# A gated linear-attention block on one core: the first phase in another order, its weight rounds spread anew, the attention's tiles reordered

## The chip, the core and the metric

The kernel runs on one core of a Trainium2 chip. The metric is the device time of one execution in microseconds (us); beside it stands the median over repeated runs. The engines are called as in the profile: PE (TensorE, matrix products), PEld (its weight loads), DVE (VectorE), ACT (ScalarE), POOL (GpSimd) and SP (SyncE, which here issues nearly all DMA transfers). Every engine works its own queue in order; so does SP, and a transfer that must wait for its data holds up those issued behind it.

## What is computed

The reference, cut to what matters, with x of 2048 x 576, 32 heads of 18 and a hidden width of 4608:

```python
xn = layernorm(x)                                   # eps 1e-5, no scale
q, k, v = split_heads(xn @ wqkv)                    # wqkv 576 x 1728
phi = lambda t: where(t > 0, t + 1, exp(t)) + 1e-6
kv = einsum("bhsd,bhse->bhde", phi(k), v)           # one state for all tokens
z  = einsum("bhsd->bhd", phi(k))
o  = einsum("bhqd,bhde->bhqe", phi(q), kv) / (einsum("bhqd,bhd->bhq", phi(q), z)[..., None] + 1e-6)
s  = merge_heads(o) @ wo                            # wo 576 x 576
g  = silu(gelu(x @ w1 + b1) @ w2 + b2)              # w1 576 x 4608, w2 4608 x 576
out = x + s * g
```

The state needs all tokens before any output of the attention can be formed: first a pass over all tokens (phase 1), then the attention tile by tile, then the two-layer network (FFN), which takes most of the time.

## The kernel before

**Products.** Every fp32 operand of a product is split into a rounded high part (a cast, mostly on ACT) and a low part (raw minus high, mostly on DVE); a product is done as high x high, low x high and high x low. The large products use a seven-product scheme on 2 x 2 blocks: sums and differences of blocks are formed for both operands, seven products replace eight, and the results are put together from PSUM. `ORDER_X` (line 149) gives the order of the products of a token pair: 2, 1, "e2", "sa", 6, "sb", "e5", 7, 5, 4, 3, where "e2" and "e5" are remainders of the contraction and "sa", "sb" are the state products (phi(k) times v) of the pair before.

**Phase 1 (lines 540 to 1111).** The 2048 tokens are 16 tiles of 128 in 8 pairs. Pairs 0 and 1 are written out by hand (648 to 745) as eight plain products, x00 to x11, with the loads, the splits of wqkv (`split_w`, 316), the sums of wqkv's blocks (`w_sum`, 322: T3, T1, T2, T4, two halves each, on POOL) and their rounding (`w_hi`, `w_lo`, 329 to 336) between them. Pairs 2 to 7 go through `phase1_pair` (868) and `products` (802). `products` issues the matmuls in the order above and calls a hook after each; the hooks carry the other work: for the pair itself phi of k (`phi_hi` three ACT operations, `phi_max` on DVE), the adds that put k, v and q together, and three `snapshot`s (800, ACT copies of a PSUM bank that the next product then overwrites, so PE waits for them). For the coming pairs the steps of preparation are: `load_x` (tile of x), `statistics` (189, DVE; the power on POOL), `share_stats` (230, mean and 1/deviation stored to DRAM), `load_stats` (234, read back as a broadcast tile bc), `load_xt` (245, the transposed x into R, which has two buffers), `center` (253, POOL subtracts the mean), `scale` (257, DVE), `x_sums` (263, DVE), the rounding `rest_hi`/`x_hi_ops` (ACT) and `rest_lo`/`x_lo_ops` (DVE), and the stores `store_rest`, `store_ops` (1792 KB of operands a pair, used again by the FFN). In pairs 6 and 7 only k and v are computed; their q products follow as `products(6, "q")` and `products(7, "q")` (981 to 1111).

When pair p runs, in the kernel before, statistics are made for pair p + 2 in the hook "e2", centring for pair p + 2 in hook 7, scaling, sums and rounding for pair p + 1 in hooks 2 to "sb". Pair 2 is an exception: most steps for pair 3 run in its own hooks 7 and 5.

**Weight rounds (460 to 538).** Between its other work the kernel prepares operands of the FFN's weights and stores them to DRAM: 5 We rounds (load 256 KB, store 896 KB) and 9 W2 rounds (load 864 KB, store two times 576 KB). A round is load, `round_sums` (POOL in phase 1, DVE in the attention), `round_hi` (ACT), `round_lo` (DVE), `round_store`, which also issues the next load. The raw tile has one buffer, so the rounds are one chain. Phase 1 does one round in each of pairs 3 to 7 (sums after product 1, hi after "sb", lo and store after 7) and one in the q products; the attention does sums at even tiles j, the rest at odd ones (1451 to 1454).

**Transition (1049 to 1164).** `make_zb` and `fold_wo` fold wo into the state; `split_kw` (1162) rounds the result into kw_h and kw_l. The last state product, the masking of the state and the first tiles' q handling stand here. zb, a broadcast row of sums that POOL multiplies with q (`by_sums`), is copied on POOL behind two tiles' work.

**Attention (1166 to 1457).** Tile j, in the order of tiles `TO`, is one pass of `attend(j)`: 28 matmuls, a copy of the result, a store. Around it stand the load of q for j + 6, the transposition of p for j + 2 (`transpose_p`, PE, with ACT and DVE rounding it to th and tl), and by_sums, denominators and p_mult for j + 4. For the four first tiles (`RAW`) phi of q was not applied in phase 1 and is done here, four tiles ahead. `beside(j)` (1392) loads and prepares the FFN's first operands at fixed j, and the weight rounds run as above. `TO` is 12, 13, 0 to 11, 14, 15.

**FFN (1845 to 1955).** 18 steps of up and down products; the change touches none of it.

Of the kernel before, what the change touches and what calls it, by code (L numbers as in the profile page):

```python
# [24 lines left out]
KT = 5  # L25
# [22 lines left out]
def linear_attention_gated_ffn(ctx, tc, x, xT, wqkv, wo, w1, w1e, b1, w2, b2, out):  # L48
# [272 lines left out]

    def w_sum(name, k, eng):
# [4 lines left out]
        eng.tensor_tensor(raw_w[name][:, k], raw_w[a][:, k], raw_w[b][:, k], op=op)  # L327
# [161 lines left out]
    class WeRound:  # L489
# [21 lines left out]
        def store(self):  # L511
# [5 lines left out]
    rounds = [WeRound(0), W2Round(0), WeRound(1), W2Round(1), WeRound(2), W2Round(2), WeRound(3),  # L517
              W2Round(3), WeRound(4)] + [W2Round(c) for c in range(4, NC)]
# [39 lines left out]
    for t in (3, 4, 5):  # L558
        load_x(t)
# [71 lines left out]
    def sums_plain_lo(p):  # L631
        x_lo_ops(p, 2, 10)
        store_ops(p)
# [11 lines left out]
    dve, pool = nc.vector, nc.gpsimd  # L645

# [16 lines left out]
    normalize(1)  # L663
    transpose_x(1)
# [19 lines left out]
    tile_raw(1)  # L684
# [9 lines left out]
    w_sum("T1", 0, pool), w_sum("T1", 1, pool)  # L694
# [10 lines left out]
    load_xt(2)  # L705
    for t in (6, 7, 8, 9):
        load_x(t)
    w_sum("T2", 0, pool), w_sum("T2", 1, pool)
# [8 lines left out]
    store_rest(1)  # L717
    statistics(6), share_stats(6), statistics(7), share_stats(7)
    center(2)
    load_stats(6), load_stats(7)  # L720
    w_sum("T4", 0, pool), w_sum("T4", 1, pool)
# [5 lines left out]
    scale(2)  # L727
    x_sums(2)
    w_hi("T2", 0), w_hi("T2", 1)
    w_lo("T2", 0, dve), w_lo("T2", 1, dve)  # L730
    k11 = phi_plain(3, x12)
    k11()
    op_tiles(2)
    x13 = bank2("x13")
    plain_x(1, 1, 1, x13, THEN)
    rest_hi(2), x_hi_ops(2, 0, 14)
    rest_lo(2), x_lo_ops(2, 10, 14)
    values_plain(3, x13)
    x11 = bank2("x11")
    plain_x(1, 0, 1, x11, THEN)  # L740
    x_lo_ops(2, 0, 10)
    store_rest(2), store_ops(2)
    w_hi("T3", 0), w_hi("T3", 1)
    w_lo("T3", 0, dve), w_lo("T3", 1, dve)
# [57 lines left out]
    def products(p, part, hooks, before=None):  # L802
# [8 lines left out]
        for i in ORDER_X:  # L811
# [15 lines left out]
            elif i == "e5":  # L827
# [3 lines left out]
                if kv:  # L831
                    nc.vector.tensor_tensor(
                        as2(k_bufs[0]), kv_of(X0), as2(u)[:, :, :KV], op=ADD
                    )
                    phi_hi(f"k{p}0", as2(k_bufs[0]))
                if q:
                    add_q(T0, 0, X0, u, part)
            elif i == 7:
                product_x(p, 7, A, part, False, rest=False)
                snapshot(p, 0, A, part)  # L840
                if kv:
                    phi_max(f"k{p}0", k_bufs[0], as2(k_bufs[0]))
            elif i == 5:
# [3 lines left out]
                if q:  # L847
                    add_q(T1, 1, X1, u_all[p][0], part)
            elif i == 4:
# [18 lines left out]
    def phase1_pair(p):  # L868
# [3 lines left out]
        nxt = p + 2 if p + 2 < NPR else None  # L872
        qp = (2 * p - 2, 2 * p - 1) if 2 < p < NPR - 1 else ()

        def operands():
            scale(prep)
            store_rest(prep)
            x_sums(prep)
            op_tiles(prep)

        def operands_hi():
            rest_hi(prep), x_hi_ops(prep, 0, 14)

        def operands_lo():
            x_lo_ops(prep, 0, 7), x_lo_ops(prep, 7, 14)
            store_ops(prep)

        def next_statistics():
            if nxt:
                ts = 2 * nxt, 2 * nxt + 1  # L890
                for t in ts:
                    statistics(t), share_stats(t)
                for t in ts:
                    load_stats(t)

        steady = prep is not None and not first

        def h2():
            if steady:
                operands()  # L900
            if first:
                x_sums(1, rest=False)
            if qp:
                phi_q_hi(qp[0])

        def h1():
            if steady:
                operands_hi()
            if first:
                x_hi_ops(1, 2, 10)  # L910
                w_hi("T1", 0), w_hi("T1", 1)
            if qp:
                phi_q_max(qp[0]), store_q(qp[0])
            if p in ROUNDS:
                round_sums()

        def he2():
            if not first:
                next_statistics()
            else:  # L920
                sums_plain_lo(1)
                load_xt(3), load_xt(4)

        def hsa():
            if steady:
                rest_lo(prep)
            if first:
                w_lo("T1", 0, dve), w_lo("T1", 1, dve)

        def hsb():  # L930
            if steady:
                operands_lo()
            if first:
                w_hi("T4", 0), w_hi("T4", 1)
                w_lo("T4", 0, pool), w_lo("T4", 1, pool)
                center(3)
            if p in ROUNDS:
                round_hi()

        def h7():  # L940
            if nxt and not first:
                center(nxt)
            if first:
                operands()
                operands_hi()
            if p in ROUNDS:
                round_lo(), round_store()

        def h5():
            if qp:  # L950
                phi_q_hi(qp[1]), phi_q_max(qp[1]), store_q(qp[1])
            if first:
                rest_lo(prep), operands_lo()
                next_statistics()
# [3 lines left out]
        def h4():  # L958
            if first:
                center(nxt)  # L960
                round_load()

        if p + 3 < NPR:
            load_x(2 * p + 6), load_x(2 * p + 7)
        if nxt and not first:
            load_xt(nxt)
        if p >= NPR - 2:
            late_tiles(p + 2)
        if not first:
            pend.pop()()  # L970
        products(p, part, {
            2: h2, 1: h1, "e2": he2, "sa": hsa, "sb": hsb, 7: h7, 5: h5, 4: h4,
        }, p - 1)

    ROUNDS = range(3, NPR)
# [4 lines left out]

    pend.pop()()
# [3 lines left out]
    op_tiles(NPR)  # L985
    f = OPS[NPR].bitcast(F32).rearrange("p a b -> p (a b)")
    wo_sb = late["wo"] + [f[:, :D]]
    nc.sync.dma_start(wo_sb[4][: GROUPS[4][1]], wo[GROUPS[4][0] :, :])
    nc.sync.dma_start(b1c, b1)
    TO = [2 * NPR - 4, 2 * NPR - 3, *range(2 * NPR - 4), 2 * NPR - 2, 2 * NPR - 1]  # L990
    for i in range(2):
        q_of[i] = f[:, (i + 1) * D : (i + 2) * D]
        nc.sync.dma_start(q_of[i], q_dram[i])
    state(NPR - 1)
    kvz, sums_k, last_row, zb_first = (late[n] for n in ("kvz", "sums_k", "last_row", "zb"))
    mask = late["mask"]
    ln = GROUPS[-1][1]
    nc.vector.copy_predicated(kvz[:G, : 4 * G], mask[:G, :], ps_kv[0][:G, : 4 * G])
    nc.vector.copy_predicated(kvz[:ln, 4 * G : D], mask[:ln, :ln], ps_kv[1][:ln, :ln])
    nc.vector.copy_predicated(kvz[:ln, D:], mask[:ln, 8:ln], ps_kv[1][:ln, 8:ln])  # L1000
# [1012 lines left out]
```

## Time and profile before

| what | value |
|---|---|
| runs of the kernel, us | 1228.76, 1224.53; median 1226.64 |
| profiled execution, us | 1229.29 |
| its span, us | 1227.6 |
| mean granted clock of PE | 0.951 |
| DMA over the span | 284.93 MB, mean 232 GB/s |

The profile is of one execution. Its lines give busy times of each engine, what ended an engine's idle time (`<-` names the releaser, with the tile and the line), and the clock that the throttle granted to PE. In a timeline a row is start, length, engine, line, operation, output and inputs, and in brackets the idle time before it. In rows of groups the two numbers behind the bar are the total busy time in us and the mean of one in ns. A span's stage is read by cutting it where PE begins the next pair.

### The profile page before, as it was taken

Reading aid. Unit: us, or ns where it says so; the run is one execution under the profiler, and the core shown is the slowest. Engines: PE = TensorE matmul, PEld = TensorE weight load, DVE = VectorE, ACT = ScalarE, POOL = GpSimd, SP = SyncE. Lnnn points to the kernel's source line nnn. Section 1 sums busy time; section 2 is a strip of 40 time slices with the busy share of each in tenths; the row PEclk is TensorE's granted clock in tenths of the full one; section 3 lists DMA queues with packets and bytes.
Section 4 is the critical chain, followed back from the end, with each engine's and each line's share of the span. In section 5 each row is a group of like instructions: output and inputs, shape, how many; then the busy total and the mean of one; then the engine's idle time right before and its main releaser. Section 6 shows DMA issues by size and latency. Waiting matters only on the chain.

```text
span 1227.6 us, 17832 instructions
## 1 busy us (share of the span) xinstructions
PE 1107.6 (90%) x6492; PEld 1015.6 (83%) x6492; DVE 847.6 (69%) x1212; ACT 512.9 (42%) x858; POOL 470.5 (38%) x391
## 2 busy tenths in 40 slices
PE   7975798857545799999999999999999999999998
PEld 6875798746545598998899899899899899889988
DVE  7474775355463688888888889877557557647666
ACT  6442565435221445445445445543323323323433
POOL 4332433133321456446445544523423413413430
PEclk9988899978867899999999999999999999999999
DMA  5565668316799968657757856899777767667452
GB/s 205 151 169 152 213 199 261 135 48 207 227 345 361 344 255 316 231 190 296 269 185 262 302 182 232 304 406 357 229 255 227 228 222 221 221 217 235 156 166 104
DMA packets 121359, 284.93 MB, mean 232 GB/s; under 512 B 12598, under 2 KB 54582, under 8 KB 118712
## 3 DMA queue, kind: packets, MB, share of 16 engines
q1 hardware_dynamic: 121272, 283.80, 67.1%
q8 instruction: 51, 0.84, 0.3%
q14 instruction: 36, 0.29, 0.1%
HBM read 176.23 MB, written 106.64 MB: 230 GB/s over the span
## 4 chain that ended last, share of the span: by engine, by line
PE 65%; DMA 6%; DVE 3%; issue 2%; SPq 1%; ACT 0%; POOL 0%; DVEq 0%; ACTq 0%
PE pm L1632 31%; PE e L1493 9%; PE zy L1493 9%; PE a L1493 9%; PE b L1493 5%; DMA w2r<-w 3%; PE pd L1752 2%; DMA s_dram<-s 1%; DVE w2o L482 1%; DMA rq_dram<-wa_rest1s 0%; DMA wa_rest1q<-rr_dram 0%; DMA we<-w1e 0%; DVE den L1017 0%; DVE w2r L471 0%; DVE w2r L472 0%
## 5 line engine op out<-in xcount | busy, mean ns | idle before, releaser
L1638 DVE TENSOR_TENSOR macc<-pm,macc 128x576 f32<-128x576 f32 x218 | 163.7, 751 | 50.3 <-PE pm L1632 48.4
L1210 ACT CAST h_h<-g 128x512 fp32r<-128x512 f32 x204 | 121.8, 620 | 132.8 <-PE pm L1632 131.7
L1213 DVE TENSOR_TENSOR h_l<-g,h_h 128x512 fp32r<-128x512 f32 x204 | 161.9, 800 | 0.0
L1175 PE MATMUL ps_s<-kw_h,th 128*128 128x288 f32 x160 | 41.3, 345 | 56.5 <-DVE th L1130 45.8
L1598 POOL TENSOR_TENSOR mid<-g 128x512 f32<-128x512 f32 x34 | 44.0, 1293 | 108.9 <-ACT g L1501 108.9
L1175 PEld LDWEIGHTS ps_s<-kw_h,th 128*128 128x128 f32 x160 | 30.8, 227 | 58.3 <-issue 45.5
L1592 POOL TENSOR_TENSOR g<-g 128x512 f32<-128x512 f32 x34 | 54.9, 1615 | 49.7 <-DVE h_l L1213 28.4
L1501 ACT ACTIVATE g<-b,b1c 128x512 f32<-128x512 f32 x36 | 24.8, 690 | 102.8 <-DVE b L1519 102.7
L1256 POOL TENSOR_TENSOR w1raw<-w1raw 128x256 f32<-128x256 f32 x18 | 13.2, 736 | 128.1 <-ACT h_h L1210 68.4
L1510 ACT COPY mid<-a 128x512 f32<-128x512 f32 x36 | 21.1, 585 | 94.1 <-PE a L1493 94.1
L1493 PE MATMUL a<-h0f,wa 128*128 128x512 f32 x144 | 51.5, 398 | 5.7 <-ACT mid L1510 5.7
L1513 DVE TENSOR_TENSOR mid<-b,mid 128x512 f32<-128x512 f32 x36 | 24.8, 690 | 45.6 <-PE b L1493 39.8
L1595 POOL TENSOR_TENSOR g<-g 128x512 f32<-128x512 f32 x34 | 55.2, 1624 | 2.7
L1723 POOL TENSOR_TENSOR fin1l<-fin1h,fin1l 128x288 f32<-128x288 f32 x8 | 6.9, 866 | 117.9 <-DMA fin1l<-s_dram 42.6
L1493 PE MATMUL a<-h0r,wa 128*128 128x512 f32 x144 | 50.4, 390 | 0.0
L1213 DVE TENSOR_TENSOR h_l<-mid,h_h 128x512 fp32r<-128x512 f32 x34 | 48.9, 1439 | 1.2
L1025 POOL TENSOR_TENSOR vb<-q,den 128x576 f32<-128x576 f32 x14 | 19.3, 1377 | 74.9 <-DVE den L1021 64.6
L1501 ACT ACTIVATE g<-e,b1c 128x512 f32<-128x512 f32 x36 | 24.8, 690 | 51.3 <-DVE e L1526 51.3
L1589 POOL TENSOR_TENSOR g<-g 128x512 f32<-128x512 f32 x34 | 44.2, 1299 | 2.7
L1526 DVE TENSOR_TENSOR e<-e,mid 128x512 f32<-128x512 f32 x36 | 24.8, 690 | 22.3 <-PE e L1493 22.3
L1175 PE MATMUL ps_s<-kw_l,th 128*128 128x288 f32 x160 | 39.6, 334 | 0.0
L471 DVE TENSOR_TENSOR w2r<-w2r 128x576 f32<-128x576 f32 x6 | 4.5, 758 | 49.7 <-DMA w2r<-w 49.7
(1029 smaller groups left out, 3667.0 us busy)
## 6 DMA issues: line engine op xcount, KB each, us to landing
we<-we_dram SPq DMA_DIRECT2D x36, 448.0 KB, 3.9
x_dram<-OPS SPq DMA_DIRECT2D x8, 1792.0 KB, 8.4
w2raw<-w SPq DMA_DIRECT2D x10, 1152.0 KB
op<-w2o SPq DMA_DIRECT2D x18, 576.0 KB, 5.0
w1raw<-w SPq DMA_DIRECT2D x18, 512.0 KB, 12.1
op_a<-wa SPq DMA_DIRECT2D x18, 512.0 KB, 5.7
op_c<-wc SPq DMA_DIRECT2D x18, 512.0 KB, 9.5
op_d<-wd SPq DMA_DIRECT2D x18, 512.0 KB, 6.5
```

Of the source, the lines that this page charges most:

```text
L1175: nc.tensor.matmul(ps[:, h, :HD], st[:, k, :], w[:, k, h * HD : (h + 1) * HD], start=(i == 0), stop=(i == len(seq) - 1),)
L1210: nc.scalar.copy(pair[0], src)
L1213: eng.tensor_tensor(pair[1], src, pair[0].bitcast(F32), op=SUB)
L1493: nc.tensor.matmul(ps, st, mv, start=first and n == 0, stop=n == len(seq) - 1, skip_group_check=True,)
L1501: nc.scalar.activation(g, ps, AF.Gelu_apprx_tanh, bias=b1c[:, f : f + 1])
L1513: tt(u1_sb, B, m1_sb, op=ADD)
L1589: tt(src[5, pr], A(1, 0), A(1, 1), op=ADD)
L1592: tt(src[6, pr], src[5, pr], A(0, 0), op=SUB)
L1595: tt(src[3, pr], A(0, 1), src[6, pr], op=SUB)
L1598: tt(src[7, pr], A(0, 0), A(1, 0), op=SUB)
L1632: nc.tensor.matmul(ps[:, q, :HD], hs[p][st][:, cs], m[:, p, :], start=(n == 0 and i not in CHAIN), stop=(n == 5), skip_group_check=True,)
L1638: nc.vector.tensor_tensor(dst, src, dst, op=ADD)
```

## The change

It moves work; the arithmetic is the same except where named.

- Prologue and pairs 0, 1: loads of x from tile 5 on are issued one by one earlier; statistics are made and shared for pairs 2 and 3 earlier, and for pair 4 within pair 1 (a new helper `share`); the eight `w_sum`s and the two `w_lo` of T4 go from POOL to DVE; three splits of the second weight half are cast together ahead of tile 2's normalization; pair 1's sums and pair 2's roundings come earlier; `load_xt(2)`, `load_xt(3)` follow the operand stores; centring of pairs 2 and 3 is done here.
- Pairs 2 to 7: statistics for p + 3 in hooks 5 and 4, centring for p + 2 in hook 7, scaling and sums for p + 1 in hook 2; rounding for p + 1 in hooks 1 and "sa" for pairs 3 to 5, in "sb" and later otherwise. Phi of a k tile moves one hook later. Phi of stored q tiles: both tiles in hooks 2 and 1, for pairs 3, 4, 5 and 7.
- Weight rounds: order We0, W2-0, W2-1, We1, W2-2, W2-3, We2, We3, W2-4, We4, W2-5 to W2-8 (before: alternating to We4, then W2-4 to W2-8). A table `ROUNDS` places six whole rounds at (pair, hook); the seventh's sums stand in q product 6. In the attention the sums stand at odd j, the rest at even j.
- Transition: the last state products and the mask go into q product 6; zb's copy goes to ACT; `split_kw` is interleaved with the transpositions, and the denominators of tiles 2 and 3 come after the first two splits.
- Attention: `TO` is 13, 12, 4 to 11, 0 to 3, 14, 15.

```diff
-    for t in (3, 4, 5):
+    for t in (3, 4):
         load_x(t)
...
+    def share(t):
+        statistics(t), share_stats(t)
...
     k00 = phi_plain(0, x00)
+    for k in (0, 1, 4):
+        w_hi_plain(k, 1)
     normalize(2)
-    tile_raw(0)
+    load_x(6)
+    tile_raw(0), tile_raw(1)
     k00()
-    split_w(0, 1, dve)
-    statistics(3), offset(3)
-    split_w(1, 1, dve), split_w(4, 1, dve)
+    w_lo_plain(0, 1, dve)
+    statistics(3)
+    w_lo_plain(1, 1, dve), w_lo_plain(4, 1, dve)
+    offset(3)
+    share(4), share(5)
...
-    w_sum("T3", 0, pool), w_sum("T3", 1, pool)
     sums_plain(0)
     tile_hi(2)
+    normalize(3)
+    load_x(7)
+    load_x(8), load_x(9)
     k01()
...
+    load_stats(4), load_stats(5)
+    w_sum("T3", 0, dve), w_sum("T3", 1, dve)
+    sums_plain_hi(0)
     values_plain(1, x01)
-    sums_plain_hi(0)
-    statistics(4), share_stats(4), statistics(5), share_stats(5)
-    normalize(3)
+    w_sum("T1", 0, dve)
     sums_plain_lo(0)
-    load_stats(4), load_stats(5)
+    center(2)
+    w_sum("T1", 1, dve)
+    w_sum("T2", 0, dve), w_sum("T2", 1, dve)
...
+    QP = {p: (2 * p - 2, 2 * p - 1) for p in range(3, NPR - 2)}
+    QP[NPR - 1] = (2 * NPR - 6, 2 * NPR - 5)
+    SUMS, HI, END = (round_sums,), (round_hi,), (round_lo, round_store)
+    ROUNDS = {
+        (3, 2): SUMS, (3, "sb"): HI, (3, "e5"): END,
+        (3, 5): SUMS, (4, "q"): HI, (4, 1): END,
+        (4, "e5"): SUMS, (4, 7): HI, (4, 5): END,
+        (5, 2): SUMS, (5, "sb"): HI, (5, "e5"): END,
+        (5, 5): SUMS, (6, 2): HI, (6, 1): END,
+        (6, "e5"): SUMS, (7, "q"): HI, (7, 1): END,
+    }
...
-    TO = [2 * NPR - 4, 2 * NPR - 3, *range(2 * NPR - 4), 2 * NPR - 2, 2 * NPR - 1]
+    TO = [2 * NPR - 3, 2 * NPR - 4, *range(4, 2 * NPR - 4), *range(4), 2 * NPR - 2, 2 * NPR - 1]
...
-    products(NPR - 2, "q", {2: round_sums, 7: lambda: (round_hi(), round_lo(), round_store())})
+    products(NPR - 2, "q", {2: round_sums, "sb": masked_state, 4: first_phi}, NPR - 1)
...
-    nc.gpsimd.tensor_copy(zb[1], zb_first)
+    nc.scalar.copy(zb[1], zb_first)
...
-        if loaded and j % 2 == 0:
+        if loaded and j % 2:
             round_sums(dve)
         elif loaded:
             round_hi(), round_lo(), round_store()
```

The hooks of `phase1_pair`, after:

```python
def h2():
    if first: w_hi("T4", 0), w_hi("T4", 1)
    if prep: scale(prep), store_rest(prep), x_sums(prep), op_tiles(prep)
    for n, t in enumerate(qp[::-1]):
        phi_q_hi(t)
        if not n: rounds_at(p, "q")
def h1():
    if early: rest_hi(prep), x_hi_ops(prep, 0, 14)
    for t in qp[::-1]: phi_q_max(t), store_q(t)
def hsa():
    if first: w_lo("T4", 0, dve), w_lo("T4", 1, dve)
    if early: rest_lo(prep), x_lo_ops(prep, 0, 7), x_lo_ops(prep, 7, 14)
def hsb():
    if prep and not early: rest_hi(prep), x_hi_ops(prep, 0, 14)
def h7():
    if cent: center(cent)                 # cent = p + 2
    if early: store_ops(prep)
def h5():
    if stat: share(2 * stat), share(2 * stat + 1)   # stat = p + 3; then load_x of the next pair
def h4():
    if stat: load_stats(2 * stat), load_stats(2 * stat + 1)
    if first: round_load()
```

`load_xt(p + 2)` stands at the start of pair p, and `early` is true for pairs 3 to 5.

More of the change, by code (lines that the diff above doesn't have):

```diff
@@ L917, in he2 @@
[L917 to L932, printed above, removed]
+        cent = p + 2 if p + 2 < NPR else None
+        stat = p + 3 if p + 3 < NPR else None
+        qp = QP.get(p, ())
@@ L933, in hsb @@
+        early = 2 < p < NPR - 2
+        def h2():
             if first:
                 w_hi("T4", 0), w_hi("T4", 1)
[L935 to L938, printed above, removed]
-        def h7():
[L941 to L947, printed above, removed]
@@ new lines, in hsa, with hsb, he5 @@
+        def hsa():
+            if first:
+                w_lo("T4", 0, dve), w_lo("T4", 1, dve)
+            if early:
+                rest_lo(prep), x_lo_ops(prep, 0, 7), x_lo_ops(prep, 7, 14)
+        def hsb():
+            if prep and not early:
+                rest_hi(prep), x_hi_ops(prep, 0, 14)
+        def he5():
+            if first:
+                rest_lo(prep), x_lo_ops(prep, 0, 7), x_lo_ops(prep, 7, 14)
+                store_ops(prep)
+        def h7():
+            if cent:
+                center(cent)
+            if early:
+                store_ops(prep)
@@ L958, in h4 @@
         def h4():
+            if stat:
+                load_stats(2 * stat), load_stats(2 * stat + 1)
             if first:
-                center(nxt)
                 round_load()
[L963 to L966, printed above, removed]
+        if cent:
+            load_xt(cent)
         if p >= NPR - 2:
@@ L1420, in beside @@
                 w.hi(i), w.lo(i)
[L1422 to L1425 removed]
     RAW = range(4)
+    split_kw(0, dve)
+    transpose_p(0)
+    split_kw(1, dve)
+    transpose_p(1)
+    denominators(2), p_mult(2)
+    for k in range(2, KT):
+        split_kw(k, dve)
+    denominators(3), p_mult(3)
     load_q(4), load_q(5)
[L1430 to L1431 removed]
     pad(2)
```

192 lines of the change are left out of this document (87 added, 105 removed).

## The prediction

> **What bounds the kernel now.** I read the page first, then the span cut into stages by TensorE's work (the windows view), then TensorE's waits before 430 us, and last the timelines and the chain where those waits lie.
>
> ```profile
> span 1227.6 us, 17832 instructions
> PE 1107.6 (90%) x6492; PEld 1015.6 (83%) x6492; DVE 847.6 (69%) x1212; ACT 512.9 (42%) x858; POOL 470.5 (38%) x391
> ```
>
> TensorE is busy 90% of the span, so 120 us of it are idle. The windows say where; each row is a stretch, its length, busy time of PE, PEld, DVE, ACT and POOL, granted clock, DMA share and GB/s.
>
> ```profile
> 0.00:38.94 38.94, 32.05 (x147) 27.63 (x148) 30.26 (x49) 21.58 (x39) 17.99 (x21) 0.91 0.44 161
> 38.94:73.04 34.10, 25.41 (x138) 23.43 (x137) 16.93 (x27) 13.68 (x27) 15.22 (x10) 0.95 0.53 143
> 73.04:107.66 34.62, 25.97 (x121) 24.20 (x121) 22.82 (x39) 16.06 (x24) 7.74 (x6) 0.80 0.62 193
> 107.66:143.52 35.86, 24.09 (x121) 22.41 (x120) 16.65 (x33) 14.31 (x20) 12.12 (x11) 0.81 0.63 170
> 143.52:165.49 21.97, 21.97 (x122) 20.99 (x120) 16.61 (x34) 14.52 (x21) 8.52 (x6) 1.00 0.76 241
> 165.49:187.45 21.96, 21.96 (x121) 20.99 (x120) 15.54 (x33) 14.33 (x20) 6.59 (x8) 1.00 0.77 242
> 187.45:208.06 20.61, 17.29 (x121) 17.05 (x120) 14.57 (x23) 13.45 (x20) 7.42 (x19) 0.92 0.72 231
> 208.06:223.71 15.65, 15.65 (x123) 15.49 (x121) 4.74 (x8) 6.84 (x11) 1.75 (x4) 1.00 0.59 197
> 223.71:254.50 30.79, 26.14 (x150) 21.88 (x149) 13.02 (x27) 12.21 (x28) 8.01 (x6) 0.94 0.40 130
> 254.50:269.31 14.81, 1.48 (x12) 1.05 (x10) 6.67 (x14) 6.32 (x11) 5.74 (x5) 0.71 0.14 43
> 269.31:331.20 61.89, 46.87 (x297) 44.66 (x297) 36.22 (x63) 26.78 (x48) 21.69 (x15) 0.88 0.57 183
> 331.20:414.06 82.86, 43.87 (x249) 41.37 (x249) 39.33 (x54) 17.19 (x32) 18.69 (x14) 0.75 0.94 342
> 437.46:482.18 44.72, 44.72 (x269) 40.80 (x268) 39.18 (x52) 21.28 (x38) 23.44 (x20) 1.00 0.74 279
> ```
>
> The first two rows are the prologue and pairs 0 and 1 (the plain products); then one row for each of pairs 2 to 7, one for the two late q products, one for the transition, two for the attention, and one of the 18 FFN steps. Pairs 4 and 5 show the floor: the 121 matmuls of a whole pair take 21.97 us with TensorE full and the clock at 1.00. Pairs 2 and 3 take 34.62 and 35.86 for the same work. In the FFN TensorE is full: the change leaves it alone, so what is saved ahead of it reaches the end unshortened.
>
> ```profile
> PE ps_s L1175 <- DVE th L1130: 45.8, 8, 14.3
> PE xaall L361 <- ACT u L800: 11.8, 1, 11.8
> PE ps_s L1175 <- ACT kw_h L1163: 10.7, 1, 10.7
> PE x1all L361 <- DVE q L428: 8.6, 1, 8.6
> PE x0all L361 <- DVE kph L403: 6.7, 1, 6.7
> ```
>
> Those are TensorE's longest waits before 430 us (total, times, longest). The engine named is the last link; the timelines say what held it.
>
> ```profile
> 57.35 0.46 DVE L191 BATCH_NORM_STATS2 st<-x 128x6 f32<-128x288 f32 x1 [12.20 <-DMA x<-x]
> 96.38 2.89 DVE L259 TENSOR_TENSOR R<-R,bc 128x640 f32<-128x640 f32 x2 [6.11 <-DMA R<-xT]
> 120.38 3.82 POOL L255 TENSOR_TENSOR R<-R,bc 128x640 f32<-128x640 f32 x2 [12.22 <-DMA bc<-st_dram]
> ```
>
> VectorE's queue is in order. Ahead of pair 2 it stood 12.20 us on the load of a tile of x, in pair 2 6.11 us on the transposed x of pair 3, and in pair 3 GpSimd's centring stood 12.22 us on the broadcast statistics: three loads asked for too late, with TensorE behind each.
>
> **The change, part by part.**
>
> *Start of pair 2.* The loads of x are issued earlier, so the 12.20 goes. Against that, eight weight sums and two roundings move from GpSimd to VectorE.
>
> ```profile
> L327 POOL TENSOR_TENSOR raw<-raw,raw 128x864 f32<-128x864 f32 x8 | 19.1, 2415 | 0.0
> L320 DVE TENSOR_TENSOR wB22l<-raw,wB22h 128x864 fp32r<-128x864 f32 x2 | 2.0, 1054 | 0.0
> ```
>
> On GpSimd a sum of this shape takes 2.415 us, on VectorE 1.054 by the undisturbed row, so ten cost VectorE 10.5 us, eight of them (8.4) ahead of pair 2. By TensorE alone pair 2 can start at 32.05 + 25.41 = 57.5. VectorE does 30.26 + 16.93 = 47.2 there; with 8.4 that is 55.6, and to 58.5 with what comes forward from pair 2. I take 58.5 instead of 73.04, a gain of 14.5; the bound on the other side is 64, if half of VectorE's 12.20 returns on other loads.
>
> *Pair 2.* Transposed loads and centring come two pairs ahead, so the 6.11 goes. VectorE's work there is 22.82, plus two roundings, 2.1, minus what went ahead: about 24 against TensorE's 22. I take 24, so pair 3 starts at 82.5 (before: 107.66).
>
> *Pair 3.* Statistics are stored and read back three pairs ahead, not two; the 12.22 is covered by a whole pair, 21.97. I take 23 instead of 35.86; pair 4 starts at 105.5.
>
> *Pairs 4 and 5.* Here nothing was to gain and something is added. The weight rounds go from one a pair to six in three and a half pairs, with their sums on GpSimd ahead of the centring and their casts on ScalarE ahead of the snapshots for which TensorE waits. The transfers exist in before; only their times move. For two rounds whose load may land late in the pair I add 0.5 and 2.5; the bounds are 0 and 2.5 for each pair. Pair 6 then starts at 105.5 + 43.9 + 3 = 152.5 (before: 187.45).
>
> *Pairs 6, 7 and the q products.* Pair 6 does pair 7's work in 17.29 busy at clock 0.92; I take 15.65 + 1, then 15.65 for pair 7, and 26.5 for the q products, whose TensorE work is 26.14. The end is at 211 instead of 254.50: **−43.5**. If TensorE never waited it would be 57.5 + 4 × 21.97 + 2 × 15.65 + 26.14 = 203, −51.5; with 64, two pairs of 26, two of 24.5, 18, 16 and 28 it is 227, −27.5.
>
> *DMA issues that move.* Seven tiles of x go to SP earlier, in stretches whose DMA share is 0.44 and 0.53; half of the engines' time covers them. SP is in order: a statistics store that waits for VectorE holds the loads behind it, which is why the bound of 64 stands.
>
> *Transition.* Its 14.81 us hold 1.48 of TensorE.
>
> ```profile
> 268.59 0.67 ACT L1163 CAST kw_h<-kw 128x576 fp32r<-128x576 f32 x1 [7.19 <-POOL zb L1143]
> ```
>
> The first cast of kw stood 7.19 us behind a copy at the tail of GpSimd's queue, which itself came behind two tiles' phi and denominators. After, that copy is ScalarE's, the denominators come later, and the masked state moves under the q product of pair 6. What stays ahead of the first attention product is a transposition and the first casts, 0.67 each: about 3 us, so **−12** (bounds −7.2, the wait alone, and −12.5).
>
> *Attention.* Three things, on rows of the chain that ends at the first FFN step, of TensorE's timeline, and of the DMA issues (KB each, us to landing).
>
> ```profile
> 331.20 9.76 DMA w2r<-w
> 352.33 9.64 DMA w2r<-w
> 374.67 10.84 DMA w2r<-w
> 392.16 6.16 DMA w2r<-w
> 407.87 6.10 DMA w2r<-w
> 421.45 3.29 PE e L1493 x7
> ```
> ```profile
> 285.99 0.51 PE L1175 MATMUL ps_s<-kw_h,th 128*128 128x288 f32 x2 [0.81 <-DVE th L1130]
> 296.29 0.82 PE L1175 MATMUL ps_s<-kw_h,th 128*128 128x288 f32 x2 [1.66 <-DVE th L1130]
> ```
> ```profile
> op<-w2o SPq DMA_DIRECT2D x18, 576.0 KB, 5.0
> w2r<-w SPq DMA_DIRECT2D x9, 864.0 KB, 6.9
> we_dram<-weo SPq DMA_DIRECT2D x5, 896.0 KB, 8.1
> we<-w1e SPq DMA_DIRECT2D x5, 256.0 KB
> ```
>
> The last five W2 rounds are a serial chain (one buffer): load, sums on an even tile, split and stores on the odd one, next load. From load to load it takes 21.1, 22.3, 17.5 and 15.7 us, mean 19.2, for two tiles. The change ends the last round at tile 14 instead of 15: one tile of the chain, −9.6. From its load's landing, 407.87 + 6.10 = 413.97, to the first FFN product are 7.5 us of VectorE and GpSimd work queued behind the load; with a tile between, about 5 of them go. The phi of the four first tiles goes from the head of the attention to tiles 6 to 9: one tile's first product is at 285.99, the next one's at 296.29, 10.3 us, where TensorE needs about 5.4 (297 of the attention's 546 matmuls, so 8.7 of its 16 tiles, in 46.87), so −5. One W2 round (864 + 2 × 576 = 2016 KB) is replaced by a We round (256 + 896 = 1152): 864 KB less, at the 408 GB/s of the row below 2.2 us. Together 9.6 + 5 + 5 + 2.2, **−22**.
>
> The transport bounds this. The stretch 331.20 to 414.06 has a DMA share of 0.94. The weak bound is its idle 6% (5.0) and the 2.2: −7. The strong one: in the whole attention the engines are busy 0.57 × 61.89 + 0.94 × 82.86, about 113, and some 6 more to the first FFN product at 421.45, 119 of 152; with transfers packed from the start −33, with the bytes −35. I take −22, between them, since the head's 43% of free DMA time is where the rounds move.
>
> ```profile
> 335.00:345.00 10.00, 1.29 (x5) 1.32 (x6) 3.79 (x7) 2.48 (x4) 0.00 (x0) 0.50 1.01 408
> ```
>
> This row shows 408 GB/s over 10 us, the engines full. The Trainium skill ("DMA: Bandwidth & Descriptors", section "Where 436 GB/s comes from") says that between HBM and SBUF some 358 GB/s bind; the row passes that, and the same page's section "Measured (HBM→SBUF, 128 partitions, SWDGE, issued from GpSimd)" has 425 for one core streaming alone. By 358 the 342 GB/s of that stretch leave 4%, an estimate of 3.7 us to gain, and the sum would be that of the first rival; by 408 they leave 16%, 13 us.
>
> *Sum.* −43.5 − 12 − 22 = −77.5, against the profiled execution's 1229.29 (span 1227.6): 1151.8. That execution stands 2.65 above the median of 1226.64, so the same sum on the median is 1149; I say **1152**.
>
> **Rivals.**
> 1. *The attention is transport-bound, and gives the earlier start back.* For: the share of 0.94. Against: the head's 0.57. Then −43.5 − 12 − 7 = −62.5, **1167**.
> 2. *Everything fits.* For: pairs 4 and 5 already run without a wait. Against: VectorE is near full ahead of pair 3. −51.5 − 12.5 − 35 = −99, **1130**.
> 3. *VectorE becomes the bound of the start.* To pair 3 it has 47.2 + 22.8 + 10.5 = 80.5 us of work, and idled 25.9 in its first 73. If half of that idling stays, pair 3 starts at 93, 11 later, a wait of some 4 in each of the next two pairs follows, and 19 are lost: −58.5, **1171**; with the bound of 2.5 in pairs 4 and 5 as well, and pair 6 slower by 4, 1180.
> 4. *The other side: a round stalls the in-order queues.* The sums stand on GpSimd ahead of the centring that the next pair needs, the casts on ScalarE ahead of the snapshots TensorE waits for, and each needs its load. If each of the six loads landed so late that TensorE stood, the gain would be gone at 77.5 / 6 = 13 us each; 2% slower (1251) needs 99.4 / 6 = 17. Against: a W2 load lands 6.9 us after its issue, and six rounds in three and a half pairs leave each some 12. Price at 18 each: 108 − 77.5, **1260**.
> 5. *The change does little:* the same mechanism at some 8 us each (48), with the attention giving nothing: −7.5, **1222**.
>
> **How the numbers follow.** Forecast 0.50, first rival 0.20, second 0.12, third 0.10, fourth 0.04, fifth 0.04. The forecast's own range is 1138 to 1164. The range of 1122 to 1186 holds the first four cases with their bounds, and leaves out the last two and tails. About 2% is what a measurement of this kernel can tell from no change: from 1202 to 1251. Faster by that 0.92, within 0.04, slower 0.04.
>
> **What would show it.** In the profile after: pair 2's first product near 58 and pair 3's near 82; seven stretches of 22 to 24 and 16 us with a clock of 1.00 up to 211; no wait of more than 3 us for bc, xT or x on VectorE and GpSimd; first attention product within 4 us of the end of the q products; the first FFN product near 344, some 130 us after the first of the attention; then 18 steps of 44.72. It is wrong if VectorE is over 95% busy ahead of pair 3, if GpSimd or ScalarE stand on the loads of the rounds while TensorE waits for u, or if the attention's stretch keeps its 150 us at a DMA share near 0.95.

## The result, and the profile after

The changed kernel takes 1167.66 us (runs of 1167.43 and 1167.89) against 1226.64; the ratio is 0.952, interval 0.945 to 0.959. Beside the later experiments it was measured again: 1171.6 against 1229.7, ratio 0.953 (0.952 to 0.955); 1167 to 1169 had been expected of that second time. The profiled execution's span is 1166.2 us, 61.4 less than before. The forecast was 1152, 16 us too low: right in sign and inside the range of 1122 to 1186, but outside the forecast's own 1138 to 1164, and on the time that the first rival gave.

The stages of the changed kernel, cut where TensorE starts the next one. Columns: length, busy time of PE, PEld, DVE, ACT, POOL, granted clock, DMA share, GB/s.

```profile
0.00:57.52 57.52, 54.09 (x284) 49.44 (x285) 50.26 (x92) 39.37 (x70) 14.55 (x22) 1.00 0.67 213
57.52:79.49 21.97, 21.97 (x122) 20.99 (x120) 19.46 (x40) 12.54 (x20) 6.08 (x4) 1.00 0.79 219
79.49:108.38 28.89, 23.77 (x122) 22.06 (x120) 17.11 (x33) 14.30 (x21) 11.71 (x12) 0.94 0.83 239
108.38:131.21 22.83, 22.17 (x122) 21.07 (x121) 16.64 (x33) 11.76 (x17) 3.33 (x2) 1.00 1.03 266
131.21:161.59 30.38, 24.42 (x121) 22.85 (x120) 17.67 (x27) 17.94 (x26) 14.88 (x13) 0.89 0.75 227
161.59:177.07 15.48, 15.48 (x122) 15.47 (x120) 11.47 (x20) 9.26 (x14) 4.11 (x4) 1.00 0.70 235
177.07:195.18 18.11, 15.69 (x122) 15.46 (x121) 9.67 (x13) 11.40 (x18) 6.31 (x18) 1.00 0.75 239
195.18:219.88 24.70, 23.72 (x150) 20.33 (x149) 10.96 (x25) 11.81 (x27) 6.53 (x8) 1.00 0.22 74
219.88:221.72 1.84, 1.27 (x13) 1.03 (x11) 1.07 (x2) 1.47 (x4) 0.41 (x2) 1.00 0.78 219
221.72:351.05 129.33, 85.43 (x518) 82.13 (x519) 74.19 (x124) 47.54 (x85) 47.32 (x33) 0.82 0.84 298
351.05:375.50 24.45, 22.92 (x100) 18.16 (x99) 20.03 (x28) 14.98 (x25) 12.12 (x10) 1.00 0.95 362
375.50:420.22 44.72, 44.48 (x266) 40.48 (x265) 39.16 (x53) 21.27 (x37) 23.41 (x20) 1.00 0.81 305
```

For the last stages of the kernel before, cut in the same way (all 16 attention tiles; then from the first product of the FFN to its first down product, the FFN's head):

```profile
269.31:404.05 134.74, 83.87 (x519) 81.05 (x520) 71.00 (x113) 40.94 (x75) 37.58 (x28) 0.79 0.78 275
404.05:437.30 33.25, 26.07 (x100) 20.13 (x99) 23.38 (x31) 17.78 (x31) 15.28 (x13) 0.85 0.94 352
```

| stage | before | after | moved | forecast |
|---|---|---|---|---|
| to pair 2 | 73.04 | 57.52 | -15.5 | -14.5 |
| pair 2 | 34.62 | 21.97 | -12.7 | -10.6 |
| pair 3 | 35.86 | 28.89 | -7.0 | -12.9 |
| pairs 4 and 5 | 43.93 | 53.21 | +9.3 | +3 |
| pairs 6 and 7 | 36.26 | 33.59 | -2.7 | -4.0 |
| late q products | 30.79 | 24.70 | -6.1 | -4.3 |
| transition | 14.81 | 1.84 | -13.0 | -12 |
| attention tiles | 134.74 | 129.33 | -5.4 | -17 |
| FFN's head | 33.25 | 24.45 | -8.8 | -5 |

The moves sum to 61.8 and the FFN's steps are what they were (44.72). The shortfall lies in pairs 3 and 5 and in the attention's tiles. In the second profile of the changed kernel pair 2 starts at 57.48, pair 3 takes 29.37 (29 to 32 had been expected), pair 5 31.63, the tiles 131.41 and the head 23.85; so the tiles differ by some 2 us from one profile to the next. TensorE's waits of phase 1 in the changed kernel:

```profile
PE xaall L368 <- DVE kph L410: 6.0, 1, 6.0
PE xaall L368 <- ACT u L824: 5.8, 2, 5.1
PE x0kv L368 <- DVE OPS L277: 2.4, 1, 2.4
```

Followed back by the timelines, the 5.1 of pair 3, in order from SP to TensorE (start, length, in brackets the idle before):

```profile
85.54 1.07 SPq L232 DMA_DIRECT2D st_dram<-mv  x2
90.51 0.80 SPq L237 DMA_DIRECT2D bc<-st_dram  x2
91.36 0.42 SPq L502 DMA_DIRECT2D we<-w1e  x1
```
```profile
97.01 1.80 POOL L508 TENSOR_TENSOR we<-we 128x128 f32<-128x128 f32 x4 [10.77 <-DMA we<-w1e]
```
```profile
98.85 0.94 ACT L512 CAST weo<-we 128x896 fp32r<-128x896 f32 x1 [8.41 <-POOL we L508]
```
```profile
100.62 1.09 PE L368 MATMUL xaall<-wT4h,OPS 128*128 128x432 f32 x2 [5.12 <-ACT u L824]
```

The first round's load stands on SP behind the statistics' store and its reading back, and goes out at 91.36, in the middle of pair 3. (The store itself had waited 5.7 us for GpSimd's power, which ran behind a centring begun at 81.27.) GpSimd has stood 10.77 on it, ScalarE's cast 8.41 on GpSimd, and behind that cast stands the snapshot for which TensorE waits. Pair 5 has the same picture with a W2 round, first on SP, then GpSimd, ScalarE, VectorE and TensorE:

```profile
105.28 6.76 SPq L232 DMA_DIRECT2D st_dram<-mv  x2
124.36 0.56 SPq L473 DMA_DIRECT2D w2r<-w  x1
```
```profile
132.91 1.41 POOL L478 TENSOR_TENSOR w2r<-w2r 128x576 f32<-128x576 f32 x1 [20.75 <-DMA w2r<-w]
```
```profile
134.35 0.67 ACT L485 CAST w2o<-w2r 128x576 fp32r<-128x576 f32 x1 [8.60 <-POOL w2r L478]
```
```profile
135.06 3.39 DVE L489 TENSOR_TENSOR w2o<-w2r,w2o 128x576 fp32r<-128x576 f32 x2 [5.73 <-ACT w2o L485]
138.89 0.76 DVE L410 SCALAR_TENSOR_TENSOR kph<-xaall,ek 128x576 f32<-128x576 f32 x1 [0.45 <-ACT q L440]
```
```profile
139.71 1.09 PE L368 MATMUL xaall<-wB11h,OPS 128*128 128x432 f32 x2 [5.96 <-DVE kph L410]
```

The W2 load goes out at 124.36 and has landed by 132.91, when GpSimd's sums can begin. The cast stands 8.60, and ScalarE's part of phi of k stands behind it; VectorE does the round's roundings ahead of its own part, waits another 0.45 us for ScalarE, and only then frees TensorE's bank. This is the mechanism of the prediction's fourth rival, on two rounds of six.

SP has by then lost 6.7 us on two statistics stores. The profile's list of waits puts this down to a round sum on GpSimd, but the powers that the stores need ran at 104.71 and 105.87, ahead of that sum (108.75). The first store alone holds SP from 105.28 to 111.55, behind the issues of a round's store, a W2 load and the operands' store (101.31 to 103.43), and the engines of the DMA are full meanwhile (share 1.04, 338 GB/s). In the run with the statistics two pairs ahead (below) a load of x stands at that place, which needs no power, and holds SP longer still:

```profile
102.75 9.54 SPq L183 DMA_DIRECT2D x<-x  x2
```

So here SP stood on its own issues with the transport full, not on GpSimd; what in the queue sets these 6 to 9 us was not taken apart.

### The profile page after: what moved, and what is told of

The parts are those of the page before. It is cut to its first block, busy times and chain, and to the rows that moved or that the text cites. A ratio compares the mean times of both kernels' runs of the same rounds, so it can differ in the third digit from the quotient of the medians.

```text
span 1166.2 us, 17826 instructions
## 1 busy us (share of the span) xinstructions
PE 1096.7 (94%) x6492; PEld 1008.2 (86%) x6492; DVE 844.9 (72%) x1220; ACT 513.4 (44%) x859; POOL 453.9 (39%) x382
## 4 chain that ended last, share of the span: by engine, by line
PE 68%; DMA 5%; DVE 2%; issue 0%; SPq 0%; ACT 0%; DVEq 0%
PE pm L1644 33%; PE a L1505 10%; PE e L1505 10%; PE zy L1505 10%; PE b L1505 5%; DMA w2r<-w 3%; PE pd L1764 2%; DMA q<-q_dram 1%; DVE w2o L489 1%; DMA h0f<-x_dram 1%; DMA wa_rest1q<-rr_dram 1%; DMA s2f<-x_dram 0%; DMA s_dram<-s 0%; DVE w2r L478 0%; DVE wa_rest1ef L1356 0%
## 5 line engine op out<-in xcount | busy, mean ns | idle before, releaser
L1036 POOL TENSOR_TENSOR vb<-q,den 128x576 f32<-128x576 f32 x16 | 23.0, 1436 | 49.1 <-DVE den L1032 33.5
L255 POOL TENSOR_TENSOR R<-R,bc 128x640 f32<-128x640 f32 x12 | 22.3, 1879 | 43.3 <-DMA R<-xT 25.9
```

## The experiments

Each edits the changed kernel in one place or in the few that are named, and is measured beside the kernel before on the same chip (three chips in all); its ratio is to be held against the changed kernel's own 0.953 (0.952 to 0.955), a hundredth being some 12 us.

**The first load early.**

```diff
 def h2():
+    if first: round_load()
 def h4():
-    if first: round_load()
```

> The changed kernel with one edit: the load of the first weight round is issued in hook 2 of pair 2 instead of hook 4. Theory A (a late first load starts a cascade: GpSimd's sums hold its power and centring, the power holds the statistics stores on SP, SP holds the next rounds' loads): the waits of 5.1 us in pair 3 and of 6.0 in pair 5 both go, 12 to 15 us with the clock, so 1153 to 1156. Theory B (each round stalls by its own place): only pair 3's goes, about 7, so 1161. Theory C (the attention's transport gives all of it back): 1166 or more, with an earlier first attention product.

Ratio 0.950 (0.948 to 0.953), 1168.7 us: some 4 us less by the ratios, whose intervals overlap. Its pairs 3, 4 and 5:

```profile
79.74:103.50 23.76, 22.20 (x121) 20.93 (x120) 18.60 (x33) 14.32 (x21) 11.86 (x12) 1.00 0.96 284
103.50:129.98 26.48, 23.77 (x122) 22.55 (x120) 17.57 (x33) 11.76 (x17) 2.93 (x3) 0.94 0.97 275
129.98:158.64 28.66, 24.38 (x122) 22.83 (x121) 17.87 (x27) 17.95 (x26) 13.71 (x12) 0.88 0.73 207
```

Pair 3's wait is gone (28.89 to 23.76), but pair 4 has one of its own now (22.83 to 26.48) and pair 5 keeps most of its. Theory A's cascade is not it: the powers again run (101.71, 102.68) before the round sums (106.35), and a statistics store still holds SP 7.1 us from 102.28. B is not it wholly: the next dense round catches the stall. The time alone would fit theory C as well; the run with both edits at once (below) speaks against it.

**The rounds of the attention on the tiles of before.**

```diff
-    products(NPR - 2, "q", {2: round_sums, "sb": masked_state, 4: first_phi}, NPR - 1)
+    products(NPR - 2, "q", {"sb": masked_state, 4: first_phi}, NPR - 1)
...
-        if loaded and j % 2:
+        if loaded and j % 2 == 0:
```

> The changed kernel with the attention's rounds on the tiles of before: the seventh round's sums leave q product 6 and stand at tile 0, sums at even tiles, the rest at odd ones, so the last round ends at tile 15. The prediction's term (one tile of the chain 9.6, and 5 behind the last load): 14.6 slower, 1182. Transport theory (the engines of the DMA set the pace, only the work behind the last load counts): 5 to 9 slower, 1173 to 1177. Neither: 1168.

Ratio 0.961 (0.958 to 0.964), 1180.8 us: some 9 us dearer. Attention tiles and head:

```profile
224.28:354.52 130.24, 84.01 (x519) 80.57 (x519) 76.36 (x126) 44.97 (x81) 42.58 (x32) 0.82 0.82 284
354.52:386.87 32.35, 24.91 (x100) 19.00 (x99) 23.62 (x31) 17.46 (x30) 14.94 (x13) 0.89 0.93 348
```

The tiles take 130.24 where the two profiles of the changed kernel have 129.33 and 131.41, the head 32.35 instead of 24.45 and 23.85. So ending the rounds one tile sooner is worth about 8 us in the head and nothing that can be told in the tiles. The time by itself lies between the two forecasts (9.5 us dearer, where 5 to 9 and 14.6 were expected); by the stages it is the transport theory's, and none of the 9.6 of the chain.

**One round a pair.**

```diff
-    ROUNDS = {(3, 2): SUMS, (3, "sb"): HI, (3, "e5"): END,
-        ...
-        (6, "e5"): SUMS, (7, "q"): HI, (7, 1): END,
-    }
+    ROUNDS = {}
+    for n in range(3, NPR):
+        ROUNDS[n, 1], ROUNDS[n, "sb"], ROUNDS[n, 7] = SUMS, HI, END
```

and, as in the run above, the tiles of before in the attention, with one whole round in q product 6.

> As the run with the rounds on the tiles of before, and also one round in each of pairs 3 to 7 (sums after product 1, cast after sb, the rest after 7) and one in q product 6, as in the kernel before; the order of the rounds stays. Against that run: if the denser rounds are what stalls pairs 3 and 5 (theory A or B), 10 to 14 us faster; if the stalls have another cause, within 2 us.

Ratio 0.952 (0.950 to 0.954), 1170.9 us, 10 less than the run above, as theories A and B said. Pairs 3 and 5:

```profile
79.35:110.80 31.45, 24.22 (x122) 22.43 (x121) 17.09 (x33) 14.29 (x21) 11.72 (x12) 0.89 0.95 272
132.76:154.73 21.97, 21.97 (x122) 20.99 (x120) 17.05 (x26) 14.07 (x21) 7.55 (x4) 1.00 0.74 249
```

Pair 5 is at the floor again; pair 3 is not, since its load is as late as ever (it goes out at 93.18, and GpSimd stands 12.21 us on it).

**The waiting tiles first.** `TO` with tiles 0 to 3 at places 4 to 7:

```diff
-    TO = [13, 12, *range(4, 12), *range(4), 14, 15]
+    TO = [13, 12, 4, 5, *range(4), *range(6, 12), 14, 15]
```

> The changed kernel with the four tiles whose phi is still to be made at places 4 to 7 of the attention, not 10 to 13 (the phi then falls at tiles 0 to 3, not 6 to 9). The prediction's term: 5 slower, 1173. If the move is worth nothing, since the head lost no time by it: within 2 of 1168.

Ratio 0.958 (0.955 to 0.961), 1178.6 us. The 16 tiles take 135.53 against 129.33 and 131.41: by tiles and by ratio 4 to 6 us dearer, about the term of 5. But the loss does not stay in the head. After 40 us of the attention this run has done 176 matmuls against the changed kernel's 198, after 80 us both have done 330, after 120 us 462 and 463; the difference falls in the last two tiles. What does stay behind is the transport: 271 GB/s over those 120 us against 290, some 2.3 MB less, which at the 383 GB/s of the second half (below) is an estimate of 6 us.

**Both at once: one round a pair and an early first load.** The edits of the first and third runs, one whole round in q product 6, and the seventh round's sums in q product 7 (hook 7), so that the attention keeps its rounds.

> The changed kernel with one round in each of pairs 3 to 7 and one in q product 6, the first load in hook 2 of pair 2, and the seventh round's sums in q product 7, so that the attention's rounds stay as in the changed kernel. Theory D (the dense rounds cost pairs 4 to 7 about 10 us, the late first load costs pair 3 about 6): pairs of 22 us throughout, first attention product at 207 to 209 instead of 221.7, and the attention and the head as before that at 154: 1154 to 1156. Rival (the attention's transport gives it back, as it seems to with the early load alone): 1163 to 1168.

Ratio 0.942 (0.940 to 0.943), 1157.3 us: 14 us faster than the changed kernel beside it, 72 faster than the kernel before. Its pairs 3 to 5 and its attention:

```profile
79.05:102.67 23.62, 22.20 (x122) 20.92 (x120) 18.83 (x33) 14.30 (x21) 11.86 (x12) 1.00 1.02 273
102.67:124.64 21.97, 21.97 (x122) 20.99 (x121) 17.32 (x34) 14.67 (x22) 7.76 (x6) 1.00 0.89 258
124.64:146.60 21.96, 21.96 (x121) 20.99 (x120) 14.30 (x26) 14.20 (x21) 5.82 (x4) 1.00 0.71 226
209.75:339.98 130.23, 83.61 (x519) 80.55 (x520) 74.05 (x124) 47.61 (x85) 47.19 (x33) 0.80 0.84 295
```

Theory D holds: both stalls are gone, the attention starts at 209.75 instead of 221.72, takes the 130 us that it takes elsewhere, and gives nothing back. The 1157.3 lies just above the 1154 to 1156 expected: the late q products and the transition take 29.37 here instead of 26.54.

**The weight sums on GpSimd.** All eight `w_sum`s and T4's two `w_lo`s:

```diff
-    w_sum("T3", 0, dve), w_sum("T3", 1, dve)
+    w_sum("T3", 0, pool), w_sum("T3", 1, pool)
```

> The changed kernel with the eight weight sums and the two roundings of T4 on GpSimd, as in the kernel before. The prediction priced them at 10.5 us on VectorE, hidden since TensorE needs 57.5 by itself. If GpSimd's 2.4 us each hold the centring and the casts that follow, and slow VectorE beside them: pair 2 starts 3 to 10 us later, 1171 to 1178. If they are hidden on either engine: 1168.

Ratio 0.960 (0.959 to 0.962), 1179.6 us: 8 dearer, a little more than expected. TensorE before pair 2, which now starts at 65.73; GpSimd; and one of VectorE's own sums, here and in the changed kernel:

```profile
57.41 1.09 PE L368 MATMUL x<-wB12h,OPS 128*128 128x432 f32 x2 [5.23 <-DVE kph L410]
```
```profile
43.18 6.61 POOL L334 TENSOR_TENSOR raw<-raw,raw 128x864 f32<-128x864 f32 x3
```
```profile
45.61 2.26 DVE L268 TENSOR_TENSOR R<-R 128x256 f32<-128x256 f32 x1
43.99 0.41 DVE L268 TENSOR_TENSOR R<-R 128x256 f32<-128x256 f32 x1
```

Three sums take 6.6 us on GpSimd, and beside them VectorE's sums take up to 2.27 us instead of 0.42. VectorE has the eight sums (8.0 us) less to do ahead of pair 2, yet is busy 55.38 us there against 50.26 in the changed kernel. From 38.31 to 57.35, where it frees the bank that TensorE waits for, it does not stand idle: TensorE's 5.23 us stand behind a slowed VectorE. The move to VectorE was no hidden cost but 8 us of gain.

**The loads of x late.** Tiles 6 to 9 loaded behind x03, as before:

```diff
-    load_x(6)
...
-    load_x(7)
-    load_x(8), load_x(9)
...
     values_plain(0, x03)
+    for t in (6, 7, 8, 9):
+        load_x(t)
```

> The changed kernel with the loads of tiles 6 to 9 of x back behind the product x03, as in the kernel before. The prediction's step (the 12.20 us that VectorE stood on such a load set the start of pair 2): pair 2 starts 6 to 12 us later, 1177 to 1184. If the sums on VectorE alone were what brought pair 2 forward (8.3 us in the run with the sums on GpSimd): within 2 us of 1171.

Ratio 0.959 (0.958 to 0.961), 1177.7 us: 7 dearer; pair 2 starts at 62.65, 5.1 later. VectorE stands on the tile again:

```profile
47.44 0.46 DVE L191 BATCH_NORM_STATS2 st<-x 128x6 f32<-128x288 f32 x1 [9.61 <-DMA x<-x]
```

**Without the last three W2 loads.** The last three rounds work on the raw tile of the round before, so their operands are not the reference's; their loads, 2592 KB, are left out.

```diff
-            t = tw.tile(...); nc.sync.dma_start(t, w2[self.c][:, D:])
+            if self.c > 5: t = last_w2[0]
+            else: t = tw.tile(...); nc.sync.dma_start(t, w2[self.c][:, D:])
+            last_w2[:] = [t]
```

> The changed kernel without the loads of the last three W2 rounds: they work on the sixth round's raw tile again, so their operands are not those of the reference; sums, casts, roundings and stores remain. 2592 KB less. Transport theory (the engines of the DMA set the pace of the attention's second half): 2592 KB at 383 to 408 GB/s, 6 to 7 us, 1164. Chain theory (VectorE stands on each load for its whole landing, 9 to 12 us, with TensorE behind it): 20 to 27 us, 1144 to 1151.

Ratio 0.945 (0.943 to 0.946), 1160.2 us: 10 us less, between the two forecasts and nearer the transport's. All its tiles, then those from 300 us on:

```profile
223.26:345.17 121.91, 85.22 (x519) 81.71 (x520) 78.18 (x125) 47.52 (x85) 47.38 (x33) 0.82 0.82 289
300.00:345.17 45.17, 31.97 (x189) 30.68 (x190) 30.84 (x45) 15.93 (x29) 16.20 (x13) 0.77 1.00 379
```

With three loads fewer the engines of the DMA are still full (1.00, 379 GB/s) in the second half. The tiles shrink by 7.4 against the changed kernel's 129.33 (9.5 against the 131.4 of its second profile), where the 2592 KB at 379 GB/s take 7.0. So it is the transport that paces this stretch; the chain theory's 20 to 27 is out.

**The transition's end as before.**

```diff
+    transpose_p(0)
+    by_sums(2), denominators(2), p_mult(2)
+    pad(1)
+    transpose_p(1)
+    by_sums(3), denominators(3), p_mult(3)
     ...
-    nc.scalar.copy(zb[1], zb_first)
+    nc.gpsimd.tensor_copy(zb[1], zb_first)
...
```

with the five `split_kw` behind it.

> The changed kernel with the transition's end in the order of the kernel before: first the transpositions, sums, denominators and products of tiles 2 and 3, then the copy of zb on GpSimd, then the casts of kw; the masked state stays where the change has it. The prediction's step (the casts stood 7.19 us behind GpSimd's tail; that alone is the lower bound of the term): first attention product 5 to 9 us later, 1176 to 1180. If the masked state's move made the whole gain: within 2 us of 1171.

Ratio 0.959 (0.958 to 0.961), 1178.2 us: 7 dearer. TensorE's wait for the first casts is back:

```profile
PE ps_s L1191 <- ACT kw_h L1179: 9.4, 1, 9.4
```
```profile
234.63:361.73 127.10, 85.46 (x519) 82.88 (x520) 69.83 (x114) 46.90 (x84) 40.78 (x29) 0.79 0.84 299
```

The first attention product comes at 234.63, 11 to 13 us later than in the two profiles of the changed kernel (221.72, 223.24), more than the 5 to 9 expected; the tiles then take 127.10, so 2 to 4 us of it come back.

**Statistics two pairs ahead**, in the changed kernel and in the faster version:

```diff
-    share(8), share(9)
-    load_stats(8), load_stats(9)
...
+        def he2():
+            if cent: share(2 * cent), share(2 * cent + 1), load_stats(2 * cent), load_stats(2 * cent + 1)
         def h5():
-            if stat: share(2 * stat), share(2 * stat + 1)
         def h4():
-            if stat: load_stats(2 * stat), load_stats(2 * stat + 1)
```

> The changed kernel with the statistics of pairs 4 to 7 made, stored and read back one pair later, in the hook e2 of the pair two ahead, as in the kernel before; all else stays. If the third pair of lead is what removed the 12.22 us in pair 3 (the prediction's step): centring waits for bc again, 8 to 12 us per stalled pair, 1176 or more. If what removed it was only that pair 2 is no longer an exception: within 2 us of 1168.

> The faster version (one round a pair, first load early, the seventh round's sums in q product 7) with the statistics one pair later, in e2 of the pair two ahead. Without the stalls of the dense rounds this tells the third pair of lead apart: if it is needed, pairs 2 to 4 grow by a wait of GpSimd on bc, 1162 or more; if not, within 2 us of 1157.

In the changed kernel the ratio is 0.949 (0.947 to 0.951), 1167.2 us, 4 us less, not more. In the faster version it is 0.946 (0.944 to 0.947), 1161.2 us, 4 us more. The two do not agree on the step by itself: in the first, the stall of pair 5 has moved to pair 4 and become shorter, which hides its price. The second has no such stall, and there pair 3 takes 28.26 instead of 23.62:

```profile
81.08:109.34 28.26, 24.72 (x121) 23.14 (x120) 18.55 (x33) 14.30 (x21) 11.07 (x10) 0.88 0.72 216
```
```profile
85.70 3.11 POOL L255 TENSOR_TENSOR R<-R,bc 128x640 f32<-128x640 f32 x2 [13.80 <-ACT eq L407]
90.53 0.30 ACT L282 CAST XR<-R 128x128 fp32r<-128x128 f32 x1 [3.63 <-DVE R L259]
95.69 1.09 PE L368 MATMUL xaall<-wT3h,OPS 128*128 128x432 f32 x2 [3.54 <-ACT u L822]
```

GpSimd's centring for pair 4 comes at 85.70, 4.4 us later than in the faster version (81.32); 2.0 of these are the later start of the pair (81.08 instead of 79.05). The profile names a ScalarE operation for the end of its wait, but the centring does not read that result; bc, which it does read, goes out on SP at 82.60 and takes 3.0 us to land, so bc is the likely releaser. The casts of pair 4's operands stand behind that centring on ScalarE, and the snapshot for which TensorE waits stands behind them. A later wait of GpSimd on bc (6.89 us, up to 104.10) comes after TensorE's and stalls nothing in this pair.

The third pair of lead is worth some 4 us, not 12. The edit also reorders SP, in both kernels, and what that did was not taken apart.

## Why the prediction was right, and where it failed

*Start of pair 2: right in size, by another sum.* 57.52 against 58.5. The prediction put the gain on the load of x and took the sums on VectorE for a cost that TensorE covers. Undone one at a time, the loads are worth 5.1 us and the sums 8.2. The prediction added the sums to VectorE's 47.2 and came to 55.6 and more; it measured 50.26. The run with the sums back on GpSimd shows what the sum left out: beside them VectorE's other work takes longer.

*Pair 2: right.* It runs at the floor, 21.97; no wait of TensorE is left in it.

*Pair 3: failed by 5.9.* The wait for bc went, but the first round's load came in its place. The prediction gave the lateness of rounds to pairs 4 and 5 alone and had not followed the first load through SP's queue. Its own sign of being wrong came true here: GpSimd (10.77) and ScalarE (8.41) stand on the load of a round while TensorE waits for u.

*Pairs 4 and 5: the failed step.* "0.5 and 2.5; the bounds are 0 and 2.5 for each pair." Measured +9.3. The bound was set without a row: a stall on a load there is the load's landing less its lead, and then it holds four queues. The loads stood on SP behind other issues: the first behind a store that waited 5.7 us for GpSimd's power and its reading back, the later one behind stores that SP took 6.7 us to issue while the transport was full. An early first load alone gave some 4 us, one round a pair alone 10, both together 14; with both in place, pairs 3 to 5 take 23.62, 21.97 and 21.96. So the fourth rival named the right mechanism and its right place; its count and size were off, two stalls of 5 and 6 us where it asked for six of 13.

*Transition: right.* 13.0 against 12; undoing its end gives the wait of 9.4 back and costs 7 us of the whole.

*Attention: mis-sized.* 14.2 against 22. RAW's place is worth 4 to 6, about as forecast (5), though it is paid in transfers at the end and not in the head. "One tile of the chain, −9.6" is worth nothing that can be told in the tiles, and what is queued behind the last load about 8, not 5. The chain's loads were read as a chain of latencies; by the run without the last three loads they are the visible end of a full transport, where a shorter chain gains nothing. In the second half the changed kernel shows:

```profile
300.00:350.00 50.00, 32.21 (x181) 31.12 (x182) 26.17 (x44) 15.83 (x29) 16.11 (x13) 0.78 1.01 383
```

*The first rival* had the transport right, and the time that it gave, 1167, is the one measured, but by luck, as two errors cancel: it left phase 1's 43.5 whole (34.6 were measured) and gave the attention 7 (14.2 were measured). "Gives the earlier start back" is refuted in the main: in nine profiles whose attention is as in the changed kernel the tiles start anywhere from 209.75 to 234.63 and take 127.10 to 131.41, the shortest for the latest start. That fits a stage whose transfers begin with its tiles (the DMA share is 0.22 in the late q products); no run tests this by itself.

*The third rival* did not come about. Its second time, 1180, counts the 3 us of pairs 4 and 5 twice and should be 1177.

The Trainium skill ("DMA: Bandwidth & Descriptors", section "Where 436 GB/s comes from") would bind these transfers at some 358 GB/s. The 383 over 50 us above are past that, so the rule's limit is not what stopped the gain.

## What to carry to other kernels

Before work is packed more densely into in-order queues, follow its load through the issuing queue too: here its lateness was paid by what stood behind it on GpSimd, ScalarE and VectorE, and with one spot mended the next dense place stalled. Before a wait that ends on the same kind of load again and again is read as a chain of latencies, look at the share of the transfer engines in that very stretch. Undo the parts one by one even where the sum came out, for a term can be right in size for the wrong reason. And where the profile names a releaser, compare its end with the start of what it is said to release: in two places here it was another, or probably was.

## What the runs showed of the hardware

A short gap can cost more than itself. After TensorE had stood for 1.92 us in pair 3 of the changed kernel with statistics two ahead, pairs of 128x432 products took 0.92 us instead of 0.56 for a while, at a granted clock of 0.51:

```profile
98.20 0.66 PE L368 MATMUL xaall<-wT4h,OPS 128*128 128x432 f32 x2 [1.92 <-ACT u L822]
100.81 0.92 PE L368 MATMUL xaall<-wT4l,OPS 128*128 128x432 f32 x2
102.21 0.56 PE L368 MATMUL xaall<-wRh,XR 128*128 128x432 f32 x2
```
```profile
98.70:102.20 3.50, 3.50 (x11) 3.23 (x10) 1.65 (x4) 1.49 (x3) 0.00 (x0) 0.51 0.14 10
```

The slow products begin half a microsecond after the gap and end some 3.5 later; that pair's PE time is 24.01 for the work that takes 21.97. A gap of 2.71 us (pair 4 with the first load early) does the same for 3.7 us, at a clock of 0.56. The gap of 2.4 us in pair 7 of the changed kernel cost nothing of the kind (15.69 in its row, against 15.48 in pair 6). After the longer gaps the slow stretch took 3.1 us (gap of 5.12), 5.0 (5.96) and 6.0 (5.23, with the sums on GpSimd). The Trainium skill ("TensorE: Matmul & The Clock Gate", section "What's actually happening") has half the clock after an idle window of about 3.4 us, counted on a free-running window. Three of the five slow stretches are near that length, but gaps shorter than the window were enough here, at two places and not at a third.

GpSimd's work can slow VectorE's beside it: next to GpSimd's 128x864 sums VectorE's 128x256 sums took up to 2.27 us instead of 0.42 (the run with the sums on GpSimd). There, eight sums given to GpSimd saved VectorE no time.
